# First unit's first four column tiles computed row by row, engines of PSUM copies from a table, and a new instruction order

## The chip, the cores and the metric

The kernel runs on one core of a Trainium2 chip. A core has TensorE (PE; its weight loads are listed apart as PEld), VectorE (DVE), ScalarE (ACT), GpSimd (POOL) and SyncE (SP, which issues most DMAs). They run side by side, each in the order of its own queue, and wait for each other by semaphores. The metric is the device time of one execution in microseconds (us).

## The reference

Two layers, each a gated state-space convolution (A) and a feed-forward net (B), both behind a layer norm and added to the residual stream. S = 2048 rows, D = 512, F = 1792, 4 taps.

```python
def _A_ref(q, k, v, shift_k, ssm_k, ssm_D):
    k_shift = sum(k_pad[:, t:t + S, :] * shift_k[:, ks - 1 - t] for t in range(ks))
    kv = k_shift * v
    y = irfft(rfft(kv, 2 * S) * rfft(ssm_k, 2 * S))[:S]      # causal convolution, by channel
    y = y + kv * ssm_D
    return q * y
def _B_ref(x, w_gate, w_up, w_down):
    return (silu(x @ w_gate) * (x @ w_up)) @ w_down

x = A_q
x = x + _A_ref(_layernorm(x), A_k, A_v, A_shift_k, A_ssm_k, A_ssm_D)
x = x + _B_ref(_layernorm(x), B_w_gate, B_w_up, B_w_down)
x = x + _A_ref(_layernorm(x), A_k, A_v, A_shift_k, A_ssm_k, A_ssm_D)
x = x + _B_ref(_layernorm(x), B_w_gate, B_w_up, B_w_down)
```

The convolution doesn't depend on x, so both layers use the same y.

## The kernel before

**Tiling.** The sequence is cut into four blocks c of 512 positions. A position of a block is 4p + r, with p on the partitions and r one of four rows (R = 4), so a row is a tile of 128 partitions by 512 channels. A block has two halves h; half 0 holds rows 0 and 2, half 1 rows 1 and 3. A unit is (layer, block, half): 16 units, run for each block as (0,c,0), (0,c,1), (1,c,0), (1,c,1), each with two rows of 128 positions.

**The convolution.** Block products in the frequency domain: DFT matmuls (matrix `fwd`) bring h and kv to spectra H and X, VectorE multiplies them (t) and sums them to Z, another few sums give m and a matmul with `inv` gives y (Yk). kv itself is a shift of k by four taps, done as matmuls of kTb with diagonal matrices dg (`shift_mul`), times v on VectorE. Block 0 of this must be done before the first unit can run; blocks 1 to 3 are worked off among the units.

**A unit.** `prologue` takes the normed x times y, adds it to x, takes row statistics (`ln_stats`: bnst, mv and ve on VectorE, then the inverse root as a power on GpSimd, rstd), normalises x to z and transposes z to zT: by a DMA from SP's queue for most units, by TensorE, through a PSUM tile ptz, for the first two (`on_pe`), where one copy to SBUF is ScalarE's and one VectorE's. Where ScalarE normalises it needs nmr = -mean * rstd first. `gate_up` then multiplies zT with w_gate and w_up for a group of column tiles (groups of four tiles of 128 columns of F, then a rest): for two column tiles at a time four matmuls each (KD = 4) of 128 x 256, both rows side by side, into a PSUM tile pf; ScalarE takes silu of gate into sg and copies up into ht; VectorE multiplies them into ht. `down` multiplies ht with w_down into a PSUM tile pd for each row, summed over all groups, and at the end ScalarE copies pd to dn and VectorE adds it to x.

**What sets the order.** Each operation is recorded by `Plan.add` with its engine, cost, buffers and what it reads and writes. The table `ORDER` gives each operation a place; `Plan.order` sorts by it and gives each buffer a slot, with the planner's costs, `SAME` and `CROSS` (steps between operations), `lat` (DMA landings) and `PW`, `PWA` (power steps); `Plan.issue` then emits the operations in that order. PE is filled with idle matmuls (wm) where the plan sees it wait in the first 32 us. So the engine queues follow from the table; the costs act only on which slot a buffer gets, and on the fillers. PSUM has rings pf (4 tiles), pc (2) and pd (2).

**The queues at the places that matter.** L323 is the line of the helper `mm`, which issues most matmuls, so tiles tell them apart: ps<-hs,fwd and ps<-vt,fwd are DFTs, ps<-dg,kTb the shift, pf<-zT gate and up, L994 pd<-wd_sb,ht down. L470 is the first block's DFT of kv, L809 its inverse, L935 the transposes of z, L940 and L938 the two copies to zT, L879 z or n on VectorE, L874 on ScalarE, L826 the power step, L863 nmr, L908 the transposing DMA, L536 and L527 kv, L434 a spectrum's copy out of PSUM on VectorE, L977 and L974 the ht copy and silu, L979 the ht product.

Of the kernel before, what the change touches and what calls it, by code (L numbers as in the profile page):

```python
# [23 lines left out]
PW = 1.2  # L24
# [19 lines left out]
PWA = 2.4  # L44
EVEN = True
SUMS = False
K0 = "rows"
CK0, LT0 = 3.0, 3.5
# [4 lines left out]
VE_D = False  # L53
SHARE = {(1, 0, 1): 2, (0, 2, 0): 2, (1, 3, 0): 2}
ORDER = [
# [79 lines left out]


class Op:
    __slots__ = ("eng", "cost", "lat", "emit", "bufs", "preds", "succs", "due", "fixed", "conv", "grp", "dest", "sl", "end", "start", "n")


class Plan:
# [1199 lines left out]
```

## Time and profile before

| | |
|---|---|
| median of 3 runs | 343.24 us (342.99 to 343.62) |
| profiled execution, first to last instruction (span) | 341.1 us |
| PE busy | 336.9 us, 2563 matmuls |
| VectorE busy | 282.4 us, 478 instructions |
| ScalarE busy | 252.5 us, 496 instructions |
| GpSimd busy | 37.3 us, 46 instructions |
| HBM read, written | 12.33 MB, 2.10 MB |

The span is what the profile of one execution shows; the time of a run is taken around it and is longer, 2.14 us of the median here. In the page's picture of 40 slices, below in tenths of busy time, PE is full from the second slice to the last but one, VectorE until about 260 us, and the granted clock of PE is full throughout.

```profile
PE   8999999999999999999999999999999999999996
PEld 7657858678687567768587756768685877777683
DVE  8899999999999999999999999889997533726022
ACT  7899999999977475778999973768665545545451
POOL 4000100002106100103100100101101000001000
PEclk9999999999999999999999999999999999999999
DMA  7999314050224175010110224010101110001111
```

### The profile page before, as it was taken

How to read it: one execution, taken by the hardware profiler on the slowest of the kernel's cores; microseconds unless marked ns; L12 is line 12 of the kernel's file. 1: busy time of each engine (PE TensorE's matmuls, PEld its weight loads, DVE VectorE, ACT ScalarE, POOL GpSimd, SP SyncE). 2: the span in 40 equal slices, each digit the busy share in tenths (PEclk: the TensorE clock that was granted, in tenths of full speed). 3: DMA queues.
4: the chain of work that ended last, by engine and by line, in shares of the span. 5: the costliest groups of instructions: out<-in, count | busy, mean ns of one | idle time of the engine just before them, and what ended most of it. 6: DMA issues, size and time to landing. Idle time of an engine off the chain costs nothing.

```text
span 341.1 us, 6468 instructions
## 1 busy us (share of the span) xinstructions
PE 336.9 (99%) x2563; PEld 242.8 (71%) x2563; DVE 282.4 (83%) x478; ACT 252.5 (74%) x496; POOL 37.3 (11%) x46
## 2 busy tenths in 40 slices
PE   8999999999999999999999999999999999999996
PEld 7657858678687567768587756768685877777683
DVE  8899999999999999999999999889997533726022
ACT  7899999999977475778999973768665545545451
POOL 4000100002106100103100100101101000001000
PEclk9999999999999999999999999999999999999999
DMA  7999314050224175010110224010101110001111
GB/s 280 333 320 341 52 31 63 0 156 1 34 46 94 31 102 164 3 30 2 33 20 13 48 46 125 0 33 1 33 0 44 36 33 0 17 16 21 27 33 31
DMA packets 42088, 22.95 MB, mean 67 GB/s; under 512 B 33989, under 2 KB 39882, under 8 KB 42058
## 3 DMA queue, kind: packets, MB, share of 16 engines
q1 hardware_dynamic: 41904, 22.49, 26.0%
q8 instruction: 20, 0.33, 0.4%
q14 instruction: 10, 0.08, 0.1%
q10 hardware_dynamic: 154, 0.05, 0.1%
HBM read 12.33 MB, written 2.10 MB: 42 GB/s over the span
## 4 chain that ended last, share of the span: by engine, by line
PE 94%; ACT 3%; DMA 1%; SPq 0%; issue 0%; ACTq 0%
PE pf L323 57%; PE pd L994 28%; PE ps L323 6%; PE ps L470 2%; DMA kn<-in_A_k_dram 1%; ACT H L431 1%; ACT Yk L729 1%; ACT ks L526 0%; ACT n L874 0%; PE pt L378 0%; PE pt L489 0%; ACT zT L940 0%; ACT X L431 0%; SPq L354 0%; ACT xc L1052 0%
## 5 line engine op out<-in xcount | busy, mean ns | idle before, releaser
L323 PE MATMUL pf<-zT,wg_sb 128*128 128x256 bf16 (+1 forms) x872 | 110.3, 276 | 0.0
L323 PE MATMUL pf<-zT,wu_sb 128*128 128x256 bf16 (+1 forms) x872 | 110.0, 275 | 0.1
L994 PE MATMUL pd<-wd_sb,ht 128*128 128x512 bf16 (+1 forms) x462 | 106.2, 373 | 0.0
L323 PEld LDWEIGHTS <-wu_sb 128*128 128x128 bf16 x872 | 85.3, 98 | 18.9 <-issue 0.6
L323 PEld LDWEIGHTS <-wg_sb 128*128 128x128 bf16 x872 | 85.3, 98 | 17.3
L977 ACT CAST ht<-pf 128x512 bf16<-128x512 f32 x112 | 65.0, 592 | 23.0 <-PE pf L323 22.8
L974 ACT ACTIVATE sg<-pf 128x512 bf16<-128x512 f32 x112 | 66.6, 606 | 20.8 <-PE pf L323 17.3
L994 PEld LDWEIGHTS <-ht 128*128 128x128 bf16 x462 | 45.0, 98 | 44.1
L979 DVE TENSOR_TENSOR ht<-ht,sg 128x1024 bf16<-128x1024 bf16 (+1 forms) x61 | 38.9, 642 | 19.8 <-ACT ht L977 13.7
L826 POOL TENSOR_TENSOR rstd<-ve,nhalf 128x2 f32<-128x2 f32 x24 | 25.1, 1047 | 192.6 <-DVE ve L824 192.6
L821 DVE BATCH_NORM_STATS2 bnst<-xc 128x6 f32<-128x512 bf16 x48 | 31.8, 684 | 0.5
L1075 ACT CAST dn<-pd 128x512 bf16<-128x512 f32 x30 | 17.2, 590 | 17.5 <-PE pd L994 17.5
L431 ACT ACTIVATE X<-ps 128x512 bf16<-128x512 f32 x32 | 18.9, 606 | 10.5 <-PE ps L323 10.0
L1078 DVE TENSOR_TENSOR xc<-xc,dn 128x1024 bf16<-128x1024 bf16 x15 | 10.3, 687 | 16.8 <-ACT dn L1075 16.8
L669 DVE TENSOR_TENSOR t<-X,G 128x2048 bf16<-128x2048 bf16 x18 | 21.9, 1218 | 0.1
L665 DVE TENSOR_TENSOR t<-X,G 128x2048 bf16<-128x2048 bf16 x18 | 21.9, 1219 | 0.0
L855 POOL TENSOR_TENSOR rstd<-ve,nhalf 128x2 f32<-128x2 f32 x8 | 8.4, 1052 | 78.5 <-ACT ve L853 78.5
L679 DVE TENSOR_TENSOR Z<-Z,t 128x2048 bf16<-128x2048 bf16 x12 | 14.7, 1221 | 0.3
L677 DVE TENSOR_TENSOR t<-t,t 128x2048 bf16<-128x2048 bf16 x12 | 14.6, 1220 | 0.2
L431 ACT ACTIVATE H<-ps 128x512 bf16<-128x512 f32 x24 | 14.2, 612 | 0.0
L901 DVE TENSOR_TENSOR n<-n,Yk 128x1024 bf16<-128x1024 bf16 x15 | 10.3, 690 | 3.1 <-ACT n L874 1.9
L323 PE MATMUL ps<-hs,fwd 128*128 128x512 bf16 x40 | 12.7, 379 | 0.1
(103 smaller groups left out, 321.8 us busy)
## 6 DMA issues: line engine op xcount, KB each, us to landing
hn<-in_A_ssm_k_dram SPq DMA_DIRECT2D x4, 512.0 KB, 5.5
vt<-in_A_v_dram SPq DMA_DIRECT2D x4, 512.0 KB, 5.6
xc<-in_A_q_dram SPq DMA_DIRECT2D x4, 512.0 KB, 4.9
out_dram<-xc SPq DMA_DIRECT2D x15, 128.0 KB, 1.8
wg_sb<-in_B_w_gate_dram SPq DMA_DIRECT2D x1, 1792.0 KB
wu_sb<-in_B_w_up_dram SPq DMA_DIRECT2D x1, 1792.0 KB, 8.0
wd_sb<-in_B_w_down_dram SPq DMA_DIRECT2D x1, 1280.0 KB, 11.6
kn<-in_A_k_dram SPq DMA_DIRECT2D x1, 512.0 KB, 4.3
```

The costliest lines, as they stand in the source:

```text
L323: nc.tensor.matmul(o, lhsT=lhsT, rhs=rhs, start=(n == 0), stop=(n == len(terms) - 1))
L431: add("ACT", act(D), lambda: nc.scalar.activation(out=view(), in_=ps.t[:], func=ACT.Copy, scale=scale), r=[ps], w=[(buf, keys)], conv=conv)
L665: dve(n * D, lambda t1=t1, part=part: nc.vector.tensor_mul(out=t1.t[:], in0=x.t[:, sl, 0, :], in1=g.t[:, sl, part, :]), [(x, key(slots, (0 ...
L669: dve(n * D, lambda t2=t2, part=part: nc.vector.tensor_mul(out=t2.t[:], in0=x.t[:, sl, 1, :], in1=g.t[:, sl, 1 - part, :]), [(x, key(slots ...
L679: dve(n * D, lambda t1=t1, part=part: nc.vector.tensor_add(out=z.t[:, sl, part, :], in0=z.t[:, sl, part, :], in1=t1.t[:]), [t1], [zk], con ...
L821: add("DVE", 0.6, lambda st=st, i=i: nc.vector.bn_stats(out=st.t[:], in_=xs[c].t[:, i, :]), r=[(xs[c], (i,))], w=[st])
L826: add("POOL", pw, lambda: nc.gpsimd.tensor_tensor(out=rstd.t[:], in0=ve.t[:], in1=nhalf.t[:].to_broadcast((P, n)), op=ALU.pow), r=[ve, nha ...
L974: add("ACT", act(D), lambda ps=ps, sl=sl: nc.scalar.activation(out=sg.t[:, sl], in_=ps.t[:], func=ACT.Silu), r=[ps], w=[(sg, (b,))], due=( ...
L977: add("ACT", act(D), lambda ps=ps, sl=sl: nc.scalar.copy(out=ht.t[:, sl], in_=ps.t[:]), r=[ps], w=[(ht, (b,))], due=(us[0], at, 1.5, "a"))
L979: dve(n * m * W, lambda: nc.vector.tensor_mul(out=ht.t[:], in0=ht.t[:], in1=sg.t[:]), [sg], [ht], due=(us[0], (k + n) / NF, 0.0, "h"))
L994: nc.tensor.matmul((pds[o] if not cs.start else pds[HP]).t[:, cs], lhsT=ht.t[:, q, at, o * P:(o + 1) * P], rhs=wt["d"].t[:, ft, cs], start ...
L1075: add("ACT", act(D), lambda o=o: nc.scalar.copy(out=dn.t[:, o, :], in_=pds[o].t[:]), r=[pds[o]], w=[(dn, (o,))], due=(unit, 1.0, 3.0, "h"))
```

## The change

**What it does.** (1) `ROW0`: the first unit takes its row statistics, and its power step, one row at a time, and its first group of four column tiles is computed by row: for each of the two rows and for gate and up, 16 matmuls of 128 columns into one PSUM tile that holds the four column tiles of that row, instead of 8 of 256 columns for two column tiles of both rows. (2) `copy_out` replaces the copies out of PSUM; each has a form for ScalarE (activation Copy) and one for VectorE (tensor_scalar), and the table `FLIP` names those that take the other engine than the one written. The diagonal matrices dg are chosen the same way. Among the flipped ones are the first unit's two zT copies, which swap engines, and late in the run 14 ht copies and three dn copies, which go to VectorE. (3) The planner's numbers: shorter steps between engines, shorter landings of transposing DMAs, 0.69 for every power step (`PW`, `PWA`). (4) A new `ORDER` table for all operations, searched with these numbers. `FIRST_ACT` and `VFIRST` are new switches that stand where they change nothing.

```diff
-PW = 1.2
+PW = 0.69
...
-PWA = 2.4
+PWA = 0.69
...
+FLIP = {0, 1, 2, 3, 4, 6, 11, 12, 15, 16, 21, 23, 24, 26, 29, 30, 53, 54, 55, 167, 200, 215, 216, 218, 219, 221, 222, 223, 226, 228, 230, 232, 237, 240, 244, 245, 247}
 ORDER = [
-    0, 5, 1, 2, 3, 21, 16, 6, 14, 8, 15, 66, 69, 10, 7, 9, 4, 11, 34, 12, 17, 18, 13, 19, 20, 35, 26, 120, 121, 131, 27, 30, 31, 39, 37, 40, 36, 41,
...
-    SAME = {"PE": 0.0, "DVE": 0.12, "ACT": 0.05, "POOL": 0.1, "SP": 0.0}
-    CROSS = {"PE": 0.3, "DVE": 0.2, "ACT": 0.25, "POOL": 0.15, "SP": 0.0}
+    SAME = {"PE": 0.0, "DVE": 0.12, "ACT": 0.12, "POOL": 0.1, "SP": 0.0}
+    CROSS = {"PE": 0.2, "DVE": 0.14, "ACT": 0.15, "POOL": 0.05, "SP": 0.0}
...
+        if alt is not None:
+            here, there = (eng, cost, emit), alt
+            if self.choices in FLIP:
+                here, there = there, here
+            self.choices += 1
+            (eng, cost, emit), o.alt = here, there
...
+    def copy_out(dst, src, r, w, eng="ACT", n=None, scale=1.0, cost=None, **kw):
+
+        n = n or D
+        costs = dict(cost or {"ACT": act(n), "DVE": tt1(n)})
+        forms = {"ACT": lambda: nc.scalar.activation(out=dst(), in_=src(), func=ACT.Copy, scale=scale),
+                 "DVE": lambda: nc.vector.tensor_scalar(out=dst(), in0=src(), scalar1=scale, scalar2=None, op0=ALU.mult)}
+        other = "DVE" if eng == "ACT" else "ACT"
+        return add(eng, costs[eng], forms[eng], r=r, w=w, alt=(other, costs[other], forms[other]), **kw)
...
-        st = ln_stats(c, rows, 0.85)
-        stats = plan.ops[-2]
+        if not ROW0:
+            st = ln_stats(c, rows)
+            stats = plan.ops[-2]
         done = []
         for o, i in enumerate(rows):
+            if ROW0:
+                st = ln_stats(c, (i,))
+                stats = plan.ops[-2]
             z = new("z", "z", [P, D])
...
-            if o:
-                add("DVE", 0.335, lambda pt=pt, o=o: nc.vector.tensor_copy(out=zT.t[:, :, o, :], in_=pt.t[:]), r=[pt], w=[(zT, (o,))], due=-45)
-            else:
-                add("ACT", act(D), lambda pt=pt, o=o: nc.scalar.copy(out=zT.t[:, :, o, :], in_=pt.t[:]), r=[pt], w=[(zT, (o,))], due=-45)
+            copy_out(lambda o=o: zT.t[:, :, o, :], lambda pt=pt: pt.t[:], [pt], [(zT, (o,))], "DVE" if o else "ACT",
+                     cost={"ACT": act(D), "DVE": tt2(D)}, due=-45)
...
+        if ROW0 and us == (UNITS[0],) and k == 0:
+            for o in range(HP):
+                for which in ("g", "u"):
+                    ps = new("pf", "pf", [P, D], F32)
+
+                    def go(ps=ps, o=o, which=which):
+                        for q, ft in enumerate(fts):
+                            mm(ps.t[:, q * P:(q + 1) * P], [(wt[which].t[:, kd, ft * P:(ft + 1) * P], zs[0].t[:, kd, o]) for kd in range(KD)])
+                    add("PE", pe(n * KD, P), go, r=[(zs[0], (o,)), wt[which]], w=[ps], due=(us[0], (2 * o + (which == "u")) / NF, 0.0, None))
...
+            dve(n * W, lambda: nc.vector.tensor_mul(out=ht.t[:], in0=ht.t[:], in1=sg.t[:]), [sg], [ht], due=(us[0], (k + n) / NF, 0.0, "h"))
+            return ht
```

Three places show how the queues moved. The first is VectorE's queue at the start of the first unit, from its row statistics (BN_STATS, ve) over z to the copy of a transposed row (zT<-ptz). Before:

```order
L821 BN_STATS bnst<-xc 128x6
L822 BN_AGGR mv<-bnst 128x2
L824 TENSOR_SCALAR ve<-mv 128x2
L527 TENSOR_TENSOR vt<-ks,vt 128x512 x2
L879 TENSOR_SCALAR z<-xc,mv,rstd 128x512 x2
L527 TENSOR_TENSOR vt<-ks,vt 128x512
L938 COPY zT<-ptz 128x4x128
```

and with the change:

```order
L834 BN_AGGR mv<-bnst 128x2
L836 TENSOR_SCALAR ve<-mv 128x1
L833 BN_STATS bnst<-xc 128x6
L834 BN_AGGR mv<-bnst 128x2
L836 TENSOR_SCALAR ve<-mv 128x1
L541 TENSOR_TENSOR vt<-ks,vt 128x512 x2
L891 TENSOR_SCALAR z<-xc,mv,rstd 128x512 x2
L541 TENSOR_TENSOR vt<-ks,vt 128x512
L447 TENSOR_SCALAR zT<-ptz 128x4x128
```

Each row now has its own ve, the first of them ahead of the second row's statistics; the last row, which copied row 2, now copies row 0.

The second is PE's queue from the last transpose of z into the first unit's gate and up matmuls. Before:

```order
L935 MATMUL ptz<-ident,z 128x128
L323 LDWEIGHTS fwd
L323 MATMUL ps<-vt,fwd 128x512
L323 LDWEIGHTS wu_sb
L323 MATMUL pf<-zT,wu_sb 128x256
```

and with the change:

```order
L951 MATMUL ptz<-ident,z 128x128
L338 LDWEIGHTS fwd
L338 MATMUL ps<-vt,fwd 128x512
L338 LDWEIGHTS wu_sb
L338 MATMUL pf<-zT,wu_sb 128x128
```

(the pairs of fwd and of wu_sb that repeat are left out). The two DFT matmuls still stand ahead; the matmuls behind them are half as wide, of row 0 alone.

The third is VectorE's queue ahead of the eighth unit's nmr, the step that frees its z on ScalarE (the last row of each piece). Before:

```order
L558 TENSOR_TENSOR Z<-m 128x1024
L901 TENSOR_TENSOR n<-n,Yk 128x1024
L863 SCALAR_TENSOR_TENSOR nmr<-mv,rstd 128x2
L902 TENSOR_TENSOR xc<-xc,n 128x2x512
L821 BN_STATS bnst<-xc 128x6 x2
L822 BN_AGGR mv<-bnst 128x2 x2
L824 TENSOR_SCALAR ve<-mv 128x2
L879 TENSOR_SCALAR n<-xc,sm,rstd 128x512
L558 TENSOR_TENSOR Z<-m 128x1024
L863 SCALAR_TENSOR_TENSOR nmr<-mv,rstd 128x2
```

and with the change:

```order
L913 TENSOR_TENSOR n<-n,Yk 128x1024
L572 TENSOR_TENSOR Z<-m 128x1024
L914 TENSOR_TENSOR xc<-xc,n 128x2x512
L833 BN_STATS bnst<-xc 128x6 x2
L834 BN_AGGR mv<-bnst 128x2 x2
L836 TENSOR_SCALAR ve<-mv 128x2
L875 SCALAR_TENSOR_TENSOR nmr<-mv,rstd 128x2
L891 TENSOR_SCALAR n<-xc,sm,rstd 128x512
L1011 TENSOR_TENSOR ht<-ht,sg 128x1024
L891 TENSOR_SCALAR n<-xc,sm,rstd 128x512
L875 SCALAR_TENSOR_TENSOR nmr<-mv,rstd 128x2
```

All four Z<-m steps of that inverse, an ht product and a second n now stand ahead of the nmr; before, two of the Z<-m steps, that product and that n came behind it. Counted over the whole queues up to there, VectorE has two Z<-m, one ht product, one n, one copy of X from PSUM and one ve more, and in the first block's part one dg, one hs copy and one ev copy more and one kTb copy less; PE's queue up to the eighth unit's first matmul has four pd matmuls more.

More of the change, by code (lines that the diff above doesn't have):

```diff
@@ L155, in buf, with add @@
         return b
[L157 removed]
+    def add(self, eng, cost, emit, r=(), w=(), lat=None, due=None, conv=False, slack=0.0, after=(), dest=None, alt=None):
         o = Op()
+        o.alt = None
+        if alt is not None:
[4 more added lines that the diff above has]
+            (eng, cost, emit), o.alt = here, there
         o.eng, o.cost, o.emit, o.conv, o.n = eng, cost, emit, conv, len(self.ops)
@@ L382, in transpose_k @@
             src = lambda pt=pt: pt.t[:].rearrange("d r p -> d p r")
-            if engs[dt % len(engs)] == "ACT":
-                add("ACT", 0.47, lambda src=src, dst=dst: nc.scalar.copy(out=dst(), in_=src()), r=[pt], w=[(kT[b], (dt,))])
-            else:
-                add("DVE", tt1(D), lambda src=src, dst=dst: nc.vector.tensor_copy(out=dst(), in_=src()), r=[pt],
-                    w=[(kT[b], (dt,))])
+            copy_out(dst, src, [pt], [(kT[b], (dt,))], engs[dt % len(engs)], cost={"ACT": 0.47, "DVE": tt1(D)})
         return k_in
@@ L497, in transpose_h @@
             sl = slice(rows[0], rows[-1] + 1)
-            if engs[order.index(r0) % m] == "ACT":
-                add("ACT", act(len(rows) * D), lambda pt=pt, sl=sl: nc.scalar.copy(out=hs.t[:, sl, :], in_=pt.t[:]),
-                    r=[pt], w=[(hs, rows)], conv=conv)
-            elif row0 is not None and r0 == 0:
+            if row0 is not None and r0 == 0:
                 turns[0] = add("DVE", 0.335, lambda pt=pt: nc.vector.tensor_tensor(out=hs.t[:, 0, :], in0=pt.t[:, 0, :], in1=row0.t[:],
@@ L504, in transpose_h @@
             else:
-                turns[r0] = add("DVE", 0.335, lambda pt=pt, sl=sl: nc.vector.tensor_copy(out=hs.t[:, sl, :], in_=pt.t[:]),
-                    r=[pt], w=[(hs, rows)], conv=conv)
+                turns[r0] = copy_out(lambda sl=sl: hs.t[:, sl, :], lambda pt=pt: pt.t[:], [pt], [(hs, rows)], engs[order.index(r0) % m],
+                                     cost={"ACT": act(len(rows) * D), "DVE": tt2(len(rows) * D)}, conv=conv)
         return hs
@@ L702, in inverse @@
                 r=[(z, key((r,))), inv], w=[ps], conv=True, dest=y)
-            add("ACT", act(D), lambda ps=ps, r=r: nc.scalar.copy(out=y.t[:, r, :], in_=ps.t[:]), r=[ps], w=[(y, (r,))],
-                conv=True)
+            copy_out(lambda r=r: y.t[:, r, :], lambda ps=ps: ps.t[:], [ps], [(y, (r,))], conv=True)
     def inverse_direct(k, slots_order):
@@ L724, with evacuate_y @@
     fresh = {}
-    def evacuate_y(k, rows):
+    def evacuate_y(k, rows, after=()):
         y, pss = Y[k], fresh[k]
         for r in rows:
-            add("ACT", act(D), lambda r=r: nc.scalar.activation(out=y.t[:, r, :], in_=pss[r].t[:], func=ACT.Copy, scale=2.0 if SUMS else 1.0),
-                r=[pss[r]], w=[(y, (r,))])
+            copy_out(lambda r=r: y.t[:, r, :], lambda r=r: pss[r].t[:], [pss[r]], [(y, (r,))], scale=2.0 if SUMS else 1.0, after=after)
     def inverse_rows(k):
@@ L886, in apply_norm @@
         rows = rows_of(h)
-        st = ln_stats_act(c, rows, after, (layer, c, h)) if on_act or ST1(layer, c, h) else ln_stats(c, rows)
-        nmr = shift_of(st, HP, due) if on_act or N_ACT(layer, c, h) else None
+        st = ln_stats_act(c, rows, after, (layer, c, h)) if on_act and FIRST_ACT or ST1(layer, c, h) else ln_stats(c, rows)
+        nmr = shift_of(st, HP, due) if on_act and FIRST_ACT or N_ACT(layer, c, h) else None
         n = new("n", "n", [P, HP, D], parts=HP)
@@ L976, in gate_up @@
                 else:
-                    add("ACT", act(D), lambda ps=ps, sl=sl: nc.scalar.copy(out=ht.t[:, sl], in_=ps.t[:]),
-                        r=[ps], w=[(ht, (b,))], due=(us[0], at, 1.5, "a"))
+                    copy_out(lambda sl=sl: ht.t[:, sl], lambda ps=ps: ps.t[:].rearrange("p (b m w) -> p b m w", b=per, m=m),
+                             [ps], [(ht, (b,))], due=(us[0], at, 1.5, "a"))
         dve(n * m * W, lambda: nc.vector.tensor_mul(out=ht.t[:], in0=ht.t[:], in1=sg.t[:]), [sg], [ht], due=(us[0], (k + n) / NF, 0.0, "h"))
@@ L1074, in ffn @@
             for o in range(HP):
-                add("ACT", act(D), lambda o=o: nc.scalar.copy(out=dn.t[:, o, :], in_=pds[o].t[:]), r=[pds[o]], w=[(dn, (o,))],
-                    due=(unit, 1.0, 3.0, "h"))
+                copy_out(lambda o=o: dn.t[:, o, :], lambda o=o: pds[o].t[:], [pds[o]], [(dn, (o,))], due=(unit, 1.0, 3.0, "h"))
             sl = span(rows)
@@ L1111 @@
         h0 = load_h(0, "SP", -70)
-        k0 = load_k(0, -69.9, after=[h0])
+        if VFIRST:
+            v0 = load_v(0, -69.95, after=[h0])
+            k0 = load_k(0, -69.9, after=[v0])
+        else:
+            k0 = load_k(0, -69.9, after=[h0])
     elif K0 == "dma":
@@ L1132 @@
     ph = new("s8", "ph", [P, NS, P], I32, parts=NS)
-    v0 = load_v(0, -59, after=[k0, dr])
+    if not VFIRST:
+        v0 = load_v(0, -59, after=[k0, dr])
     x0 = load_x(0, -58, after=[v0, k0])
@@ L1186 @@
             w = [(dg, (dt * KS + j,))]
-            if DGE[dt] == "A":
-                add("ACT", 0.32, lambda j=j, dt=dt: nc.scalar.activation(out=dg.t[:, dt, j, :], in_=ident.t[:], func=ACT.Copy,
-                                                                        scale=tapF.t[:, dt, j:j + 1]), r=[ident, tapF], w=w)
-            else:
-                e, q, cost = ("POOL", nc.gpsimd, 0.57) if DGE[dt] == "P" else ("DVE", nc.vector, 0.163)
-                add(e, cost, lambda j=j, dt=dt, q=q: q.tensor_scalar(out=dg.t[:, dt, j, :], in0=ident.t[:],
-                                                                    scalar1=tapF.t[:, dt, j:j + 1], scalar2=None, op0=ALU.mult),
-                    r=[ident, tapF], w=w)
+            forms = {"ACT": (0.32, lambda j=j, dt=dt: nc.scalar.activation(out=dg.t[:, dt, j, :], in_=ident.t[:], func=ACT.Copy,
+                                                                            scale=tapF.t[:, dt, j:j + 1]))}
+            for e, q, cost in (("POOL", nc.gpsimd, 0.57), ("DVE", nc.vector, 0.163)):
+                forms[e] = (cost, lambda j=j, dt=dt, q=q: q.tensor_scalar(out=dg.t[:, dt, j, :], in0=ident.t[:],
+                                                                          scalar1=tapF.t[:, dt, j:j + 1], scalar2=None, op0=ALU.mult))
+            e = {"D": "DVE", "A": "ACT", "P": "POOL"}[DGE[dt]]
+            other = {"DVE": "ACT", "ACT": "DVE", "POOL": "DVE"}[e]
+            add(e, *forms[e], r=[ident, tapF], w=w, alt=(other, *forms[other]))
     k_in = transpose_k(0, "pc", eng(KTE)) if K0 == "rows" else k0
```

50 lines of the change are left out of this document (28 added, 22 removed), and 116 rows, old and new, of the table ORDER.

## The prediction

> **What bounds the kernel now.** First the chain of waits, which follows the work that ended last back to its start:
>
> ```profile
> core 0 of [0], span 341.1 us
> by line: PE pf L323 57.4%; PE pd L994 28.4%; PE ps L323 6.0%; PE ps L470 2.0%; DMA kn<-in_A_k_dram 1.3%; ACT H L431 1.2%; ACT Yk L729 0.6%; ACT ks L526 0.5%; ACT n L874 0.4%; PE pt L378 0.3%; PE pt L489 0.3%; ACT zT L940 0.2%; ACT X L431 0.
> ```
>
> Over nine tenths of it are TensorE (PE) matmuls. A busy PE need not be a fast one, so the timeline of PE alone comes next (start, length, line, operands, count). The start of one row less the start of the row before, over that row's count, is the pace.
>
> ```profile
> 9.79 3.07 PE L323 MATMUL ps<-dg,kTb 128*128 128x128 bf16 x52
> 12.70 1.03 PE L323 MATMUL ps<-hs,fwd 128*128 128x512 bf16 x4
> 13.56 4.48 PE L470 MATMUL ps<-vt,fwd 128*128 128x512 bf16 x20
> ...
> 21.36 0.28 PE L1307 MATMUL wm<-const-bfloat16-1.0 128*128 128x128 bf16 x2
> 21.70 0.82 PE L323 MATMUL ps<-hs,fwd 128*128 128x512 bf16 x3
> ...
> 29.63 1.05 PE L323 MATMUL ps<-dg,kTb 128*128 128x128 bf16 x16
> 30.76 0.72 PE L935 MATMUL ptz<-ident,z 128*128 128x128 bf16 x8
> 31.41 0.71 PE L323 MATMUL ps<-vt,fwd 128*128 128x512 bf16 x2
> 32.23 1.91 PE L323 MATMUL pf<-zT,wu_sb 128*128 128x256 bf16 x16
> 33.98 0.38 PE L323 MATMUL ps<-vt,fwd 128*128 128x512 bf16 x1
> ```
>
> A matmul of 128 columns costs (12.70 - 9.79) / 52 = 0.056 us, of 512 (13.56 - 12.70) / 4 = 0.215, of 256 (33.98 - 32.23) / 16 = 0.109: the time goes with the columns. Against these paces the rows show where PE stood. 21.36 + 2 x 0.056 = 21.47, next row at 21.70: 0.23 us, and the two fillers before it (0.11) are no work either. 29.63 + 16 x 0.056 = 30.53, next at 30.76: 0.23. 30.76 + 0.45 = 31.21, next at 31.41: 0.20. 31.41 + 0.43 = 31.84, next at 32.23: 0.39. Together 1.16 us. Then the stretches; behind the length stand the busy time of PE, of its weight loads, of VectorE (DVE), ScalarE (ACT) and GpSimd (POOL), the granted clock and the DMA share:
>
> ```profile
> 60.00:145.00 85.00, 85.00 (x621) 60.57 (x620) 83.71 (x140) 67.98 (x130) 12.51 (x9) 1.00 0.29 63
> 145.00:170.00 25.00, 25.00 (x177) 17.08 (x175) 23.86 (x44) 21.47 (x43) 4.35 (x5) 1.00 0.11 22
> 260.00:342.00 82.00, 78.13 (x583) 56.54 (x580) 33.24 (x71) 38.09 (x70) 4.46 (x6) 1.00 0.11 27
> ```
>
> From 60 to 170 PE is busy in every microsecond at full clock, and VectorE in 107.57 of 110. So the matmuls are a floor that the change doesn't lower; 1.16 us around the first unit's start are what a better order can win there; and VectorE, two per cent behind PE, is what can take it back.
>
> **The change, part by part.**
>
> *Row by row.* The first unit's first group was 32 matmuls of 256 columns and is now 64 of 128: 64 x 0.056 - 32 x 0.109 = 3.58 - 3.49 = **+0.09**. Bounds: the pace of 0.056 is of matmuls with one weight load each, as the new ones are; if a narrow one took as long as a wide one, 64 x 0.109 = 6.98, +3.5. I take the first, of the same form and size. A page speaks against it: the Trainium skill, "TensorE: Matmul & The Clock Gate", section "Back-to-back issue gap", gives about 81 ns a matmul at 128 columns for a sustained stream of weight load and matmul. By that rule the 64 would cost an estimated 5.2 us and the sum would be 1.6 us higher; the trace disagrees, with 56 ns over 52 such pairs.
>
> *The first gate.* What the gaps from 30.5 to 32.2 hang on, VectorE's rows and then ScalarE's:
>
> ```profile
> 29.20 0.17 DVE L824 TENSOR_SCALAR ve<-mv 128x2 f32<-128x2 f32 x1
> 29.61 0.76 DVE L527 TENSOR_TENSOR vt<-ks,vt 128x512 bf16<-128x512 bf16 x2 [0.24 <-ACT ks L526]
> 30.30 0.73 DVE L879 TENSOR_SCALAR z<-xc,mv,rstd 128x512 bf16<-128x512 bf16 x2
> 30.94 0.42 DVE L527 TENSOR_TENSOR vt<-ks,vt 128x512 bf16<-128x512 bf16 x1
> 31.28 0.42 DVE L938 COPY zT<-ptz 128x512 bf16<-128x512 bf16 x1
> ```
>
> ```profile
> 31.10 0.59 ACT L526 CAST ks<-ps 128x512 bf16<-128x512 f32 x1
> 31.57 0.62 ACT L940 COPY zT<-ptz 128x512 bf16<-128x512 bf16 x1
> ```
>
> PE has both transposes done by about 31.3. VectorE's copy of row 2 ends at 31.70, but ScalarE casts ks first and ends its copy of row 0 at 32.19; PE starts at 32.23. In the change row 0's copy is VectorE's, in the place where row 2's stood, and the first 32 matmuls need row 0 alone. With z where it is, PE starts 0.04 behind 31.70, at 31.74: 0.49 earlier. ScalarE's copy of row 2 is hidden behind those 32 (1.8 us). Against it: one ve step more (0.17), and the second power step now stands right behind ve with the vt pair (0.76) queued after it on VectorE; if it waits for the pair, the second z, which PE's queue holds ahead of the first gate, comes 0.76 later less the 0.24 for which VectorE waits now. The ends are -1.16, every gap gone, and 0.17 + 0.76 - 0.24 - 0.49 = +0.20; I take **-0.45**, near the row that is replaced. Of the gap at 21.5 and its fillers (0.34 of the 1.16), gone from a queue that issues kTb matmuls there, I count **-0.1**: what PE doesn't lose there it may lose at the next wait for VectorE.
>
> *Ahead of it.* Up to the first gate PE's queue holds the same matmuls, the fillers apart. Four DFT matmuls stand ahead of the kn transposes that came first; a wait of theirs would show at once. VectorE does one dg, one hs and one ev copy more ahead of the kv products, and one kTb copy less:
>
> ```profile
> 8.03 0.69 DVE L434 TENSOR_SCALAR ev<-ps 128x512 bf16<-128x512 f32 x1
> 8.64 0.24 DVE L1192 TENSOR_SCALAR dg<-ident,tapF 128x128 bf16<-128x128 bf16 x1
> 8.80 0.68 DVE L434 TENSOR_SCALAR ev<-ps 128x512 bf16<-128x512 f32 x1
> 10.44 0.69 DVE L536 TENSOR_TENSOR vt<-ps,vt 128x512 bf16<-128x512 f32 x1 [0.96 <-PE ps L323]
> ```
>
> An hs copy is priced like the zT copy, 0.42, and a kTb copy, with its strided target, like ev: 0.24 + 0.42 + 0.69 - 0.69 = 0.66, under the 0.96 that VectorE idles before 10.44: hidden, **0**; without that cover +0.66.
>
> *The middle.* The tightest place is the eighth of sixteen units:
>
> ```profile
> 156.16 0.69 DVE L979 TENSOR_TENSOR ht<-ht,sg 128x1024 bf16<-128x1024 bf16 x1 [0.56 <-ACT ht L977]
> ...
> 164.21 2.50 SPq L908 DMA_TRANSPOSE zT<-z  x2
> ...
> 169.18 1.04 PE L323 MATMUL pf<-zT,wu_sb 128*128 128x256 bf16 x8
> ```
>
> and, of these two transfers in the view of their tile:
>
> ```profile
> DMA to landing us min/median/max: 2.4/2.8/3.2
> ```
>
> The second is issued at 164.21 + 1.25 = 165.46 and lands between 167.9 and 168.7; PE uses it at 169.18, with 0.5 to 1.3 us to spare. In the change VectorE's queue holds, ahead of the step that frees this unit's z and behind the head, two Z<-m steps of 1024 elements more, one ht product, one n, one copy of X from PSUM and one ve; PE's holds four pd matmuls more.
>
> ```profile
> L979 DVE TENSOR_TENSOR ht<-ht,sg 128x1024 bf16<-128x1024 bf16 x51 | 34.8, 685 | 19.3 <-ACT ht L977 13.5 <-ACT sg L974 5.7
> ...
> L879 DVE TENSOR_SCALAR n<-xc,mv,rstd 128x512 bf16<-128x512 bf16 x14 | 5.2, 409 | 2.6 <-POOL rstd L826 2.6
> ```
>
> 3 x 0.685 + 0.41 + 0.69 + 0.17 = 3.3. Steps in a row overlap (the two z above take 0.73, not 0.82): 0.09 for each of five makes it 2.9. Less 4 x 0.215 = 0.86 on PE, the lead shrinks by 2.0. Against it stand the 0.5 to 1.3 to spare and the 0.56 for which VectorE waited at 156.16, which falls away if it runs late. So the unit is late by 2.0 - 1.3 - 0.56 = 0.1 to 2.0 - 0.5 = 1.5, and all behind its first matmul in PE's queue waits as long. I take **+0.25**, near the lower end, since a late VectorE saves its other waits too.
>
> *The rest* I cost at nothing. Late in the run 14 ht and three dn copies go to VectorE, which is busy in 33.24 of the last 82 us; without that cover 17 x 0.69 = 11.7. ScalarE's copies become another form of the same instruction: the copies above, 0.59 and 0.62, differ by 0.03, and a hundred make 3 us where it idles 17 of 85 from 60 to 145. Block 2's v loads earlier on SP's queue, ahead of x; its wait there is for a free buffer, and the first unit needs neither. The planner's costs act through the order alone.
>
> **The sum.** 341.1 + 0.09 - 0.45 - 0.1 + 0 + 0.25 = 340.9 for the span. The median of the runs, 343.24, lies 2.14 above the profiled span, and with that the forecast is **343.0 us**.
>
> **The rivals.**
>
> *Every gap is won.* The new order closes all four with no debt in the middle: 343.24 - 1.16 + 0.09 = 342.2. For it: with PE full everywhere else, that is the only place where an order can win. Against it: three of the four gaps lie on one chain through ve, power step, z, transpose and copy, whose steps all stay.
>
> *VectorE sets the pace at the eighth unit, behind a held power step.* The planner now takes 0.69 for every power step. The trace has that as the median, and one of nine times that:
>
> ```profile
> L826 POOL TENSOR_TENSOR rstd<-ve,nhalf x24: 687/695/6210, 29.4 to 310.9; 128x2 f32<-128x2 f32 x24
> ```
>
> ```profile
> 105.56 6.21 POOL L826 TENSOR_TENSOR rstd<-ve,nhalf 128x2 f32<-128x2 f32 x1 [11.57 <-DVE ve L824]
> ```
>
> ```profile
> 105.60:111.00 5.40, 5.40 (x38) 3.50 (x37) 5.40 (x7) 3.15 (x6) 5.40 (x1) 1.00 0.46 96
> ```
>
> Under the long one VectorE (third time) has no free moment: seven products and sums of two SBUF tensors. The Trainium skill, "SBUF — State Buffer", section "Who interferes with whom", states that a VectorE step with two SBUF inputs and a GpSimd step that reads SBUF block each other whole; the row agrees. It did no harm there, where the unit had room. The case decides once the debt passes what the unit has to spare: a lateness of 0.8, halfway between the bounds, and a power step held by a pair like vt, 0.76, less half of the 0.56, is 1.3 late, 0.25 of which the forecast has, so 343.0 + 1.05 = 344.1; at the upper bound 1.5 + 0.76 = 2.3, 345.0. For it: the counts above. Against it: next to that unit's power step the queue also holds single-input steps.
>
> *The narrow matmuls cost what wide ones do*: 343.0 + 3.4 = 346.4. Only the bound speaks for it, the pace against it.
>
> **How the numbers follow.** Forecast, gain and debt nearly cancelling, 342.6 to 343.8: 0.42. Every gap won, 341.7 to 342.6: 0.30. VectorE's pace: 0.25. Narrow matmuls: 0.03. A run of this kernel tells 0.2%, 0.7 us, from no change and no less, so faster 0.30, same 0.42, slower 0.28. The range takes in most of the first two rivals: 341.9 to 344.6; the forecast's own stands above.
>
> **What would show it.** The first unit's first pf matmul at 31.7 to 31.8, 16 of them in 0.9 us, no gap near 21.5, PE busy in every microsecond from 60 to 145. A gap on PE before 170, ahead of a pf row whose zT landed just then, shows the debt; a power step over 1 us ahead of it, the lock. The forecast is wrong if the first gate starts at 32.2 or later, for then the chain to z has grown, or if PE stands for more than half a microsecond after 40.

## The result, and the profile after

The change took 345.47 us (median of 12 runs, 344.59 to 347.50) against 343.25 for the kernel before (12 runs, 342.89 to 345.40): a ratio of 1.0063, with a 95% interval of 1.0045 to 1.0082. It is slower, by 2.2 us or 0.6%, where 343.0 was forecast and the range ended at 344.6. The profiled execution took 345.17 us; its span is 343.4 us, against 341.1.

The page of the change, its first lines and the chain of waits by engine:

```profile
span 343.4 us, 6500 instructions
PE 335.4 (98%) x2559; PEld 242.5 (71%) x2593; DVE 292.2 (85%) x500; ACT 241.4 (70%) x476; POOL 35.6 (10%) x46
PE 70%; DVE 14%; ACT 9%; DMA 3%; issue 1%; POOL 1%; POOLq 0%
```

Before, over nine tenths of the chain was PE; now 14% of it is VectorE's and 9% ScalarE's. (34 matmul records are missing from this trace: the queue has 2593, one for each weight load.) First the start of the first unit, PE's timeline:

```profile
20.32 1.46 PE L487 MATMUL ps<-vt,fwd 128*128 128x512 bf16 x6
21.61 0.81 PE L338 MATMUL ps<-hs,fwd 128*128 128x512 bf16 x3
...
31.33 0.59 PE L338 MATMUL ps<-vt,fwd 128*128 128x512 bf16 x2
31.76 1.06 PE L338 MATMUL pf<-zT,wu_sb 128*128 128x128 bf16 x16
32.66 1.06 PE L338 MATMUL pf<-zT,wg_sb 128*128 128x128 bf16 x16
```

20.32 + 6 x 0.215 = 21.61: the gap near 21.5 and its fillers (idle matmuls) are gone. The first gate starts at 31.76 instead of 32.23, and 16 narrow matmuls take 32.66 - 31.76 = 0.90, 0.056 each. All that was forecast. Then PE's waits from 32 us to the end:

```profile
PE pf L338 <- DMA zT<-z: 0.8, 2, 0.5
PE pf L338 <- ACT ht L446: 0.5, 1, 0.5
PE pd L1026 <- DVE ht L1011: 0.4, 1, 0.4
```

The same view of the kernel before has no row. The places, on PE's timeline:

```profile
40.56 1.03 PE L1026 MATMUL pd<-wd_sb,ht 128*128 128x512 bf16 x3
42.12 0.38 PE L338 MATMUL pf<-zT,wu_sb 128*128 128x256 bf16 x2 [0.53 <-ACT ht L446]
...
68.43 1.03 PE L1026 MATMUL pd<-wd_sb,ht 128*128 128x512 bf16 x4
69.85 0.39 PE L1026 MATMUL pd<-wd_sb,ht 128*128 128x512 bf16 x1 [0.39 <-DVE ht L1011]
...
170.31 1.03 PE L1026 MATMUL pd<-wd_sb,ht 128*128 128x512 bf16 x4
171.81 0.39 PE L338 MATMUL pf<-zT,wg_sb 128*128 128x256 bf16 x2 [0.48 <-DMA zT<-z]
...
245.73 1.03 PE L1026 MATMUL pd<-wd_sb,ht 128*128 128x512 bf16 x3
247.03 0.49 PE L338 MATMUL pf<-zT,wg_sb 128*128 128x256 bf16 x3 [0.27 <-DMA zT<-z]
```

Against the pace, with the fourth pd matmul of the first and last pair, whose record is missing: 42.12 - 40.56 - 0.86 = 0.70; 69.85 - 68.43 - 0.86 = 0.56; 171.81 - 170.31 - 0.86 = 0.64; 247.03 - 245.73 - 0.86 = 0.44. With 0.18 at 124 and 0.10 at 72.6, PE stands 2.6 us after the first gate, where it stood 0.03 before. From here on **late idle** is this sum: all that PE's matmuls start later than at their pace, from the first gate to the end (2.68 in this trace, 0.03 in that of before).

So the 2.25 us between the spans are: +0.09 row by row, -0.11 fillers, -0.62 at the gaps from 12 us to the first gate (1.14 before, 0.52 now), +0.26 ahead of 12 us, where hn landed later, and +2.65 behind the first gate. (The 0.26 need not be the change's: two of the kernels below that have the order of before up to the first gate come out of the head 0.32 and 0.48 later than the kernel before in their profiled executions.)

What waits behind the first of these gaps: GpSimd, VectorE and ScalarE.

```profile
38.17 1.50 POOL L867 TENSOR_TENSOR rstd<-ve,nhalf 128x2 f32<-128x2 f32 x1 [7.70 <-ACT ve L865]
```

```profile
36.76 2.35 DVE L607 TENSOR_TENSOR G<-H,G 128x2048 bf16<-128x2048 bf16 x2
39.03 0.68 DVE L447 TENSOR_SCALAR X<-ps 128x512 bf16<-128x512 f32 x1
```

```profile
39.70 0.48 ACT L879 ACTIVATE nmr<-sm,rstd 128x1 f32<-128x1 f32 x2 [0.64 <-POOL rstd L867]
40.09 1.50 ACT L886 ACTIVATE n<-xc,nmr,rstd 128x512 bf16<-128x512 bf16 x2
41.50 0.58 ACT L446 ACTIVATE ht<-pf 128x512 bf16<-128x512 f32 x1
```

The power step takes 1.50 instead of 0.69. It stands under the second of two G products with two SBUF inputs, which ends at 36.76 + 2.35 = 39.11, and is done 0.56 later. ScalarE's queue has nmr directly behind it, then two n, and only then the ht copy that frees the PSUM tile for which PE waits. The gaps at 69 and 247 have the same step ahead of them, 1.24 and 1.50 long, with VectorE waiting:

```profile
66.61 0.69 DVE L1011 TENSOR_TENSOR ht<-ht,sg 128x1024 bf16<-128x1024 bf16 x1
67.89 0.16 DVE L875 SCALAR_TENSOR_TENSOR nmr<-mv,rstd 128x2 f32<-128x2 f32 x1 [0.58 <-POOL rstd L838]
```

```profile
240.58 1.22 DVE L679 TENSOR_TENSOR t<-X,G 128x2048 bf16<-128x2048 bf16 x1
241.71 0.17 DVE L834 BATCH_NORM_AGGREGATE mv<-bnst 128x2 f32<-128x6 f32 x1
242.38 0.41 DVE L891 TENSOR_SCALAR z<-xc,sm,rstd 128x512 bf16<-128x512 bf16 x1 [0.49 <-POOL rstd L867]
```

The Trainium skill, "SBUF — State Buffer", section "Who interferes with whom", has the rule: a GpSimd step that reads SBUF and a VectorE step with two SBUF inputs exclude each other for a whole instruction. The end times agree: 67.30 + 0.55 is the end of the step at 66.61, 241.80 + 0.54 that of the one at 240.85.

### The profile page after: what moved, and what is told of

The parts are those of the page before. It is cut to its first block, busy times and chain, and to the rows that moved or that the text cites. A ratio compares the mean times of both kernels' runs of the same rounds, so it can differ in the third digit from the quotient of the medians.

```text
span 343.4 us, 6500 instructions
## 1 busy us (share of the span) xinstructions
PE 335.4 (98%) x2559; PEld 242.5 (71%) x2593; DVE 292.2 (85%) x500; ACT 241.4 (70%) x476; POOL 35.6 (10%) x46
## 4 chain that ended last, share of the span: by engine, by line
PE 70%; DVE 14%; ACT 9%; DMA 3%; issue 1%; POOL 1%; POOLq 0%
PE pf L338 43%; PE pd L1026 20%; PE ps L338 5%; PE ps L487 2%; DVE ht L1011 2%; DVE bnst L833 2%; DMA zT<-z 2%; DVE t L683 2%; DVE t L679 1%; DVE m L566 1%; DMA hn<-in_A_ssm_k_dram 1%; DVE t L691 1%; ACT H L446 1%; ACT X L446 1%; ACT ht L446 1%
## 5 line engine op out<-in xcount | busy, mean ns | idle before, releaser
L338 PE MATMUL pf<-zT,wg_sb 128*128 128x256 bf16 (+2 forms) x888 | 109.6, 274 | 0.9 <-DMA zT<-z 0.8
L338 PE MATMUL pf<-zT,wu_sb 128*128 128x256 bf16 (+2 forms) x888 | 109.4, 274 | 0.5 <-ACT ht L446 0.5
L1026 PE MATMUL pd<-wd_sb,ht 128*128 128x512 bf16 (+2 forms) x436 | 100.9, 372 | 1.8 <-DVE ht L1011 0.4
L1006 ACT ACTIVATE sg<-pf 128x512 bf16<-128x512 f32 x110 | 64.3, 603 | 37.3 <-PE pf L338 33.6
L446 ACT ACTIVATE ht<-pf 128x512 bf16<-128x512 f32 x98 | 58.2, 604 | 28.7 <-PE pf L338 28.5
L838 POOL TENSOR_TENSOR rstd<-ve,nhalf 128x2 f32<-128x2 f32 (+1 forms) x25 | 23.8, 953 | 218.5 <-DVE ve L836 218.5
L446 ACT ACTIVATE dn<-pd 128x512 bf16<-128x512 f32 x27 | 15.8, 600 | 15.2 <-PE pd L1026 15.0
L447 DVE TENSOR_SCALAR ht<-pf 128x512 bf16<-128x512 f32 x14 | 9.5, 688 | 15.1 <-PE pf L338 15.1
L867 POOL TENSOR_TENSOR rstd<-ve,nhalf 128x2 f32<-128x2 f32 x8 | 8.9, 1111 | 56.6 <-ACT ve L865 56.6
L630 ACT ACTIVATE kc<-kTb,tapF 128x512 bf16<-128x512 bf16 x16 | 12.6, 786 | 0.0
```

The source lines that it names most:

```text
L338: nc.tensor.matmul(o, lhsT=lhsT, rhs=rhs, start=(n == 0), stop=(n == len(terms) - 1))
L446: forms = {"ACT": lambda: nc.scalar.activation(out=dst(), in_=src(), func=ACT.Copy, scale=scale), "DVE": lambda: nc.vector.tensor_scalar(o ...
L630: add("ACT", 0.66, lambda j=j, t=t, h=h, dt=dt: nc.scalar.activation(out=t.t[:, h, :, dt], in_=kT[b].t[:, dt, PADL - j:PADL - j + L].rearr ...
L838: add("POOL", pw, lambda: nc.gpsimd.tensor_tensor(out=rstd.t[:], in0=ve.t[:], in1=nhalf.t[:].to_broadcast((P, n)), op=ALU.pow), r=[ve, nha ...
L1006: add("ACT", act(D), lambda ps=ps, sl=sl: nc.scalar.activation(out=sg.t[:, sl], in_=ps.t[:], func=ACT.Silu), r=[ps], w=[(sg, (b,))], due=( ...
L1026: nc.tensor.matmul((pds[o] if not cs.start else pds[HP]).t[:, cs], lhsT=ht.t[:, q, at, o * P:(o + 1) * P], rhs=wt["d"].t[:, ft, cs], start ...
```

## The experiments

Two theories at first. **H**: a held power step, and what stands right behind it in a queue, makes PE wait. **P**: VectorE's pace sets the time, and a gap that is closed comes back further on. Two more came later: **T**, the loss is in the new order alone, which has no room; and **C**, the wide spread of the change's runs comes from its head. In each kernel everything not named is that of the change (or, where said, of the order of before).

**Three power steps freed.** VectorE's queue at the three places:

```diff
 L607 TENSOR_TENSOR G<-H,G
-L607 TENSOR_TENSOR G<-H,G
 L447 TENSOR_SCALAR X<-ps
+L607 TENSOR_TENSOR G<-H,G
...
 L836 TENSOR_SCALAR ve<-mv
-L1011 TENSOR_TENSOR ht<-ht,sg
 L875 SCALAR_TENSOR_TENSOR nmr<-mv,rstd
+L1011 TENSOR_TENSOR ht<-ht,sg x2
 L683 TENSOR_TENSOR t<-X,G
-L1011 TENSOR_TENSOR ht<-ht,sg
...
-L679 TENSOR_TENSOR t<-X,G
 L834, L891, L834, L891 (mv, z, mv, z)
+L679 TENSOR_TENSOR t<-X,G
```

> The change, with three power steps given a VectorE free of two-input steps: at 38 us the X copy from PSUM stands before the second G<-H,G, at 66 us nmr stands right behind ve and the two ht products ahead of t<-X,G, at 241 us t<-X,G stands behind the two z. PE's queue and the work are the same. Theory H (a power step that stands under a two-input VectorE step is held, and what waits for it makes PE wait): the three power steps take 0.69 instead of 1.50, 1.24 and 1.50, the gaps of PE at 41.2, 69.1 and 246.4 (0.70, 0.56 and 0.43) fall below 0.15 each, and the median is 345.47 - 1.69 = 343.8, between 343.5 and 344.1. Theory P (VectorE, with no time to spare until 200 us, sets the pace; where PE waits is chance): the gaps close but PE waits as much further on, the gap at 171 grows from 0.65 to over 1.5, and the median stays at 345.0 or above.

345.15 us, ratio 1.0054 (1.0035 to 1.0074). The three power steps take 0.69 each, and the gaps at 41 and 247 are gone. But PE's waits now read:

```profile
PE ps L338 <- ACT H L446: 0.7, 1, 0.7
PE pf L338 <- DMA zT<-z: 0.5, 1, 0.5
PE pd L1026 <- DVE ht L1011: 0.4, 1, 0.4
PE ps L338 <- DVE vt L642: 0.3, 1, 0.3
```

The wait for ht ends at 67.55 now, where the edit itself puts the product behind a wait of VectorE; PE runs into H at 124 and vt at 109 earlier than they are ready. Late idle 2.74 against 2.68: H has the mechanism right, P what becomes of the gain, though not where (the gap at 171, which P let grow to over 1.5, stays at 0.65).

**The eighth unit's chain**, which the prediction named as the tightest place.

```diff
 DVE:
+L875 nmr<-mv,rstd
 L891 n<-xc,sm,rstd
-L875 nmr<-mv,rstd
 ACT:
-L446 Yk<-ps
 L886 z<-xc,nmr,rstd
-L446 ht<-pf
+L446 Yk<-ps
 L886 z<-xc,nmr,rstd
+L446 ht<-pf
```

> The change, with the eighth unit's chain ahead of other work: its nmr stands before the second n on VectorE, and on ScalarE each of its two z stands one place earlier, before a Yk copy and before an ht copy. Theory H: the second z ends 0.5 earlier, the gap of PE at 171 falls from 0.65 to 0.15, nothing else moves, median 345.0. Theory P: the wait comes back at a later unit, median 345.3 to 345.6.

345.38 us, 1.0063 (1.0045 to 1.0082). The gap at 171 is gone and late idle falls to 2.23, nearly as H has it (the gap at 124 grows from 0.18 to 0.42). The median is the one that P has, 345.3 to 345.6, but the six runs spread from 344.37 to 346.50, and in the profiled one, 346.40, the first gate came 1.7 us later than in the change's; so the runs decide nothing.

**The two zT copies back on their engines.**

```diff
-FLIP = {..., 30, 53, 54, 55, ...}
+FLIP = {..., 30, 55, ...}
```

> The change, with the first unit's two zT copies on the engines of before (row 0 on ScalarE, row 2 on VectorE). If the first gate hangs on the copy of row 0, it starts 0.4 to 0.5 later, at 32.2 instead of 31.76. Theory H: the gap at 41.2 hangs on ScalarE's power step at 38 us and not on PE, so it gives back what the head loses: it shrinks from 0.70 to about 0.25, and the median stays at 345.5 (within 0.2). The rival, that gaps add up: median 345.9.

345.96 us, 1.0097 (1.0060 to 1.0133), spread from 344.95 to 349.42. The first gate started at 31.88, only 0.12 later than in the change: ScalarE's new queue has this copy ahead of a Yk copy, so that the swap of engines is worth little of the early gate. The gap at 41 did not shrink to 0.25, as was expected: it is 0.78, behind a power step held to 1.76. Late idle is still lower, 2.37, since the gap at 124 is gone and that at 247 is 0.27. The median decides nothing here.

**Both edits of the first two kernels.**

> The edits of e1_power and e2_unit8 together. Theory H: 345.47 - 1.69 - 0.5 = 343.3, level with the kernel before (343.1 to 343.6). Theory P: 344.6 or above.

344.47 us, 1.0037 (1.0015 to 1.0060), between the two theories; late idle 2.25, 0.8 of it in a new gap at 246, where PE waits for a dn copy.

**Where the loss is.** Three kernels made of the two orders. The first has the change's code (row by row, zT swap, new forms) in the order and on the engines of before; the second the order of before up to the first gate and the new one behind it; the third the reverse.

```diff
-ORDER = [10, 55, 2, 5, 0, ...]   FLIP = {0, 1, 2, ..., 247}
+ORDER = [the places of before]   FLIP = {53, 54}
```

> The change without its new order: rows by row in the first unit, the two zT copies swapped, the copies in their new forms, everything else in the order and on the engines of before. Theory T (the loss is in the new order alone, which leaves PE tight places with no time to spare): the first gate starts at about 31.8 instead of 32.2, PE doesn't wait after it, median 342.9, between 342.6 and 343.3, and no wider spread than before. Rival F (the narrow matmuls or the new forms of the copies cost something): median 344 or above.

> Up to the first gate the order and the engines of before (with rows by row and the zT swap), behind it the new order and its late flips. Theory T: the gaps after the first gate (2.7 us in the change) are those of the order behind it, median 344.8 to 345.5; if the wide spread of the change (344.6 to 347.5) comes from its head, where the DFT of the first spectrum stands ahead of the transposes of kn, the spread here is under 1.2 us. Rival S (the new head starts the engines on another footing, and the later gaps follow from it): median 343.5 or less.

> The head of the change with its order and engines, behind the first gate the order and the engines of before. Theory T: no gaps after the first gate, median 342.9 to 343.6, the head's own 0.26 included; if the spread comes from the head, it is over 2 us here too. Rival S: median 344.5 or above.

343.30 us (0.9999, 0.9977 to 1.0021), 345.23 (1.0058, 1.0037 to 1.0078) and 343.18 (0.9995, 0.9973 to 1.0018); late idle 0.24, 2.01 and 0.70. T holds: the new order behind the first gate costs the 2 us, whichever head stands before it, and row by row costs nothing that the runs can tell. What T had too high is the gain. In the trace of the first kernel the gate came at 32.28 and not at 31.8: PE was 0.32 late at 13 us, of which 0.27 was won back up to the gate. And 0.25 was lost at 41.4, where PE waits for an ht copy behind ScalarE's two n. That the changed code itself costs the time, or that the head does, falls with these three.

**No power step.** GpSimd fills the tile instead, which waits for ve but reads nothing (the power is left out).

```diff
-nc.gpsimd.tensor_tensor(out=rstd.t[:], in0=ve.t[:], in1=nhalf.t[:]..., op=ALU.pow)
+nc.gpsimd.memset(rstd.t[:], 1.0)
```

> The change with every power step replaced by a fill of the same tile on the same engine at the same place (the power is left out; the fill waits for VectorE's ve as the power did, but reads nothing). Theory H (a step that reads SBUF on GpSimd is held by a two-input VectorE step): the fills take no longer than the shortest power step, 0.55, everywhere; the gap at 41 (0.70), which hangs on the power step of 1.50, falls to 0.1 or less, that at 246 (0.43) too, and the median lies between 343.6 and 344.6, part of the gain being given back at 124 as in the run with three power steps moved. If writes are held like reads, the fills take 1.2 to 1.6 at the same places and the median stays at 345.5.

343.72 us (343.10 to 344.08), 0.9998 (0.9978 to 1.0018). The fills after VectorE's statistics, and those after ScalarE's:

```profile
L838 POOL MEMSET rstd<- x25: 98/99/233, 29.1 to 311.8; 128x2 f32 x23, 128x1 f32 x2
```

```profile
L867 POOL MEMSET rstd<- x8: 99/99/100, 16.9 to 240.2; 128x2 f32 x8
```

A fill is not held, under the same products. The gaps at 41, 69 and 247 are gone, the one at 170 stays, late idle is 1.34. But a fill is also shorter than the power step, so two kernels part hold and length, with 15 and with 5 fills in a row:

```diff
-nc.gpsimd.memset(rstd.t[:], 1.0)
+[nc.gpsimd.memset(rstd.t[:], 1.0) for _ in range(15)]
```

> As the run with fills, but with 15 fills in a row in place of each power step, so that it lasts about as long as a power step that is not held (0.69; the power is left out). It parts the two things that the single fill of 0.10 took away at once, the hold and the step's own length. If the hold is what costs, the median stays near that of the single fill, 343.6 to 344.2, and the gap at 41 stays under 0.2. If the length costs, it returns to 345 or above and the gap at 41 to over 0.4.

> As the run with 15 fills, which followed each other every 0.15 and lasted 2.29 instead of 0.69, now with 5 fills in place of each power step: about 0.71, the length of a power step that is not held (the power is left out). If the hold is what costs, the median stays near that of the single fill, 343.5 to 344.3; if the step's own length does, it comes to 345 or above, near the change's 345.47.

The first missed its aim: 15 fills last 2.29, one every (2.29 - 0.10) / 14 = 0.156, and the kernel took 368.82 us (1.0735, 1.0707 to 1.0763). The second lasts as long as a free power step, on GpSimd's timeline:

```profile
38.05 0.73 POOL L867 MEMSET rstd<- 128x2 f32 x5 [7.65 <-ACT rstd L865]
44.49 0.73 POOL L838 MEMSET rstd<- 128x2 f32 x5 [5.71 <-DVE rstd L836]
```

and leaves of PE's waits after the first gate one row:

```profile
PE pf L338 <- DMA zT<-z: 0.5, 1, 0.5
```

Late idle 1.11, no more than with the single fill: in the traces it is the hold and not the length that makes PE wait at 41, 69 and 247. The medians, 344.35 (1.0026, 1.0012 to 1.0041) and 343.72, lie 0.6 apart; what of that is the length and what the heads of the runs isn't settled.

**Is the order of before roomier?** The same 2.29 us steps, and a single fill, in the order of before.

> The change's code in the order of before, with 15 fills (2.29) in place of each power step (the power is left out). Theory T (the new order was made for steps of 0.69 and has no room for longer ones, the order of before has room, made as it was for 1.2 and 2.4): the order of before loses well under half of what the new order lost with the same fills (368.8 - 345.5 = 23.3), so that the median lies between 346 and 354. Rival (steps of 2.29 cost any order as much): 363 or above.

> The change's code in the order of before with one fill (0.10, not held) in place of each power step (the power is left out). Theory H': in this order the held steps, the longest of 6.21 among them, fall where other work covers them, so that taking them away gives little: 343.0 to 343.3 against 343.3 with the power steps, where the new order gained 1.75. If the holds cost the order of before as much as the new one, it comes to 341.8 or less.

364.57 us (1.0635, 1.0597 to 1.0673): 21.3 lost, against 23.3 in the new order. So T's second half falls: the order of before has hardly more room for long steps. With the single fill it takes 343.25, as with its power steps: its held ones, 6.21 among them, cost it nothing in sum. (The wait at 41.4, behind a step held to 1.50, goes, and one of 0.32 at 72 stands in its place. Beside this kernel and the next the runs of before itself spread from 343.28 to 350.41, so that no ratio is used for the two.) The two orders differ in where the held steps fall and what stands behind them.

**Fill and eighth unit together.**

> The change with one fill in place of each power step (the power is left out) and the eighth unit's chain moved ahead of other work as before: the two edits that took gaps away, together. If they are the whole loss, the gap at 170 (0.65 with the fills alone) closes and the median is 343.72 - 0.5 = 343.2, level with before; if the wait comes back at a later unit, it stays at 343.6 or above.

344.04 us (342.88 to 346.32): the median is the one that the rival has, so the runs don't bear the expectation out. The trace of the fastest of the 12 does: after 32 us PE's waits have no row, late idle is 0.33, and the page begins with the span of the kernel before:

```profile
span 341.1 us, 6499 instructions
```

VectorE's work is that of the change, 83.31 us of the 85 from 60 to 145 (82.85 in the change), so its load alone does not make PE wait. What makes the other runs of this kernel longer, 1.2 us in the median, stays open.

**The spread, and a better version.** In the third of the mixed kernels above the profiled execution took 345.12 us, at the end of its range from 342.38, and PE's timeline has the reason in the head:

```profile
3.96 0.50 PE L1343 MATMUL wm<-const-bfloat16-1.0 128*128 128x128 bf16 x3
4.82 1.90 PE L506 MATMUL pt<-ident,hn 128*128 128x128 bf16 x16 [0.36 <-DMA hn<-in_A_ssm_k_dram]
6.51 1.91 PE L338 MATMUL ps<-hs,fwd 128*128 128x512 bf16 x4
8.21 1.06 PE L393 MATMUL pt<-ident,kn 128*128 128x128 bf16 x8
```

(6.51 - 4.82) / 16 = 0.106 for 128 columns and (8.21 - 6.51) / 4 = 0.425 for 512: half the pace. It goes on behind 8.2 us, where the next 16 matmuls of 128 columns take 0.089 each. It doesn't begin with the wait for hn: the kernels' first 27 idle matmuls, from 0.76 to 3.73 us, take 0.110 each, before as with the change. What differs is when it ends. In the change's profiled execution it had ended by 4 us, and PE went on at full pace after a longer wait for hn, 0.50; in that of the single fill, where no wait for hn is listed, it lasted to 6.2. Two kernels have four idle matmuls more there, the second in the order of the third mixed kernel, with one ht copy moved between ScalarE's two n; a third tries that move in the order of before.

```diff
-n = int((start - t - (0.3 if t > 8.0 else 0.5 if t > 0.0 else 0.1)) / 0.106)
+n = int((start - t - (0.3 if t > 8.0 else 0.1 if t > 0.0 else 0.1)) / 0.106)
```

> The change with four idle matmuls more (0.106 each at half pace, 0.42) where PE waits for hn at 4.3 us. Theory C (the wide spread of the change comes from its head: PE waits for hn there, and in some runs its matmuls then go on at half pace, 0.106 for 128 columns, up to 8 us): the half pace ends before 6 us in every run, the runs lie within 1 us of each other, median 344.8 to 345.2. If the spread has another cause, it stays at 2 us or more and the median at 345.5.

> The head of the change, the order of before behind it, the ht copy moved between the two n, and four idle matmuls more at 4.3 us: the version that should beat both kernels. Theories H and C: no slow runs, median 342.6 (342.3 to 342.9). If the spread has another cause than the wait for hn: 343.1 as without the two edits.

> The change's code in the order of before, with one ht copy on ScalarE moved between the second unit's two n. In the run without that move PE reached the first gate 0.36 earlier and gave back 0.25 at 41.4, waiting for that ht copy behind two n and a power step held to 1.50. Theory H: the gap at 41.4 falls under 0.05, nothing opens later, median 343.0 against 343.3. Theory P: another gap opens, 343.3.

The change with the four idle matmuls: 345.26 us (1.0044, 1.0027 to 1.0061), just above the 344.8 to 345.2 expected, all 12 runs from 344.85 to 345.70 instead of 344.59 to 347.50. That fits C but doesn't show it: the change with the single fill has the same head without them, and its 12 runs lie as close, from 343.10 to 344.08; and the second mixed kernel, which has the head of before and should have stayed under 1.2 if the change's head were to blame, spreads by 2.29, from 344.87 to 347.16. The move alone: 343.50 (1.0005, 0.9988 to 1.0021); the gap at 41 is gone and one of 0.30 stands at 72 instead, as P has it. Head, idle matmuls and move together: 343.20 against 343.29, 0.9985 (0.9970 to 1.0000), its runs from 342.53 to 343.68. That misses the 342.3 to 342.9 that was expected and is no better than the third mixed kernel without the two edits, 343.18; in its trace the half pace lasts to 6.1 us in spite of the idle matmuls. So it is better than the change by 2 us, but that it is faster than the kernel before isn't shown, and the cause of the spread stays open.

## Why the prediction was wrong

- *The first gate, -0.45, and the gap at 21.5, -0.1*: together right and a little small, -0.62 and 0.11 of fillers. The gate came at 31.76 for 31.74. The reason given, the copy on VectorE, was mostly not the reason: with the copy back on ScalarE it came at 31.88. That it came within 0.02 is in part luck: more was won from 12 us on than was counted, and 0.26 was lost ahead of it.
- *Row by row, +0.09*: right, 0.056 a matmul; the rival of 346.4 falls.
- *The head, 0*: off by +0.26 in the profiled execution, because PE waited 0.50 for hn (0.66 after the last filler, 0.22 before). That the half pace of the start can last longer was not in the forecast at all.
- *The middle, +0.25: here it failed.* "The tightest place is the eighth of sixteen units" was right as far as it went: the gap there is 0.64, within the 0.1 to 1.5 given. But it was taken as the only place, and counted at 0.25. The others, put at nothing, cost 2.0: 0.70 at 41, 0.56 at 69, 0.44 at 247, and 0.28 at 124 and 72.6 together. The term measured 2.65. Behind the gaps at 41, 69 and 247 stood held power steps: with 5 fills, as long as a free step but not held, late idle fell to 1.11.
- *Why they were missed*: the work ahead of each unit was counted over the whole queue, with every power step at its usual length. The 6.21 us row was seen, and the hold described, but the rival that had it was placed at the eighth unit, where the step took 0.79. The question it called for was not asked of the order: which power steps become ready while VectorE is in a two-input product, and who stands behind them. The first such place can be read from VectorE's queue (two G<-H,G) and ScalarE's (nmr, n, n, then ht).
- *That rival's price*, 344.1 to 345.0, was the nearest, and still small, since it had one unit late once.
- *"Late copies cost nothing", "0 for the rest"*: no gap after 250 us exceeds a hundredth or two, so they hold.

## What to carry to other kernels

Where one engine is full and another nearly so, a total of work ahead of each deadline is not enough: list every short step on a third engine that others wait for, see what runs on VectorE when it becomes ready, and read who stands right behind it in each in-order queue. Mend such a place by the work that surrounds it, and look in the trace for where the gain is lost again before trusting the sum. Before gains of some tenths of a us are read from medians, look at how the first matmuls ran in the executions compared: here kernels with the change's order up to the first gate had that gate anywhere from 31.67 to 33.74 us in their profiled executions.

## What the runs showed of the hardware

A GpSimd fill of 128 x 2 takes 0.10 us and is not held under two-input VectorE products; a power step that reads SBUF is, until 0.55 after the product's end. Fills in a row follow each other every 0.156. TensorE's first matmuls go at half pace in these kernels, and how long that lasts differs between executions: until about 4 us in those of the kernel before and of the change, past 8 us in that of the third mixed kernel. The column of the granted clock says 1.00 all the same (third mixed kernel):

```profile
4.80:8.20 3.40, 3.38 (x20) 2.29 (x21) 2.30 (x11) 1.76 (x5) 1.48 (x4) 1.00 0.95 350
```

The change, in the same stretch, has 38 matmuls where this has 20:

```profile
4.80:8.20 3.40, 3.33 (x38) 2.52 (x40) 2.73 (x12) 2.96 (x8) 1.48 (x4) 1.00 0.94 358
```

The Trainium skill, "TensorE: Matmul & The Clock Gate", section "Part 1: The HAM clock gate (the "warmup" mystery)", describes a gate that halves the clock by recent activity over a window that runs freely; the half pace and its varying end agree. The granted clock of the profile does not show it, so the pace is to be read from starts.
